# Attention by native float32 matmuls and TensorE transposes, in place of split products and DMA transposes

## The chip, the cores and the metric

The kernel runs on one core of one Trainium2 chip. The metric is device time in microseconds (us) of one execution; less is better. The core's engines are TensorE (PE, with its weight loads as PEld), VectorE (DVE), ScalarE (ACT), GpSimd (POOL) and SyncE (SP), whose queue issues the DMAs.

## What is computed

Sliding-window attention with a linear distance penalty, then two gated blocks, all in float32:

```python
scores = q @ k.T / sqrt(64)                      # 4 batches, 8 heads, 576 positions, 64 features
rel = pos[:, None] - pos[None, :]
scores = where((rel >= 0) & (rel < 128), scores - slope[h] * abs(rel), -1e9)
attn = exp(scores - max); attn = attn / (sum + 1e-9)
x = attn @ v                                     # as 2304 tokens x 512
x = ((x @ w_a) * (x @ w_b)) @ w_out              # inner width 1536
return (((x @ w1) * (x @ w2)) @ w3) @ w_out2     # inner width 1024
```

## The kernel before

Attention goes unit by unit: a unit is one batch and two heads, 16 in all, and the two heads fill the 128 partitions with their 64 features each. Its 576 queries are five blocks i, four of 128 and a last one of 64, where both heads share the partitions. The window lets block i see keys of blocks i - 1 and i alone, so a softmax piece (one block, one head) has 128 columns for i = 0 and 256 after; the last block is one piece for both heads. `RUNS` makes three steps of a unit: blocks 0 and 1, blocks 2 and 3, block 4. "Wide" steps are the first two.

For the next unit, `prep` transposes the ten 128x128 blocks of q and k on TensorE in three parts of three, four and three (L269, with `ident`), and `parted` moves each part to SBUF as a float32r high part (ACT, L273) and the remainder (DVE, L274). `v_parts` makes three bfloat16 parts of v on GpSimd. `scores` sums three products of q's and k's parts (low x high, high x low, high x high) in PSUM (L312); for the four full blocks the two heads are two matmuls of 64 rows each, in the upper and lower half of the array. `exps` adds the bias with a running minimum of the negated score on DVE (L338) and takes exponential and row sum on ACT (L344). `norms` makes 2^15 over the row sum (L357, L360). `probs` writes the divided exponentials as float16 high part (ACT L376, for block 0 DVE L372) and float16 remainder (DVE L378), and one DMA transpose from SP's queue turns both (L383). `pv` multiplies with v stationary, head j into PSUM partitions 64 j to 64 j + 63, five products per block of keys (L409); `pv_out` writes high and low part of x (ACT L423, DVE L424).

`attention_ops` lists the order of a step n: what the last step left for late (`parted`, `pv_out`), scores and exps of step n, norms and probs of step n - 1, loads, transposes of the next unit, then at most 2.4 us worth (`FILL`) of matmuls of the first gate group, then `pv` of step n - LAG. The `Filler` may run a tile of 256 tokens only when all four units of its batch have left `pv_out` (`ready`), when the first weight group is converted, and below a cut of the accumulator (1280 tokens, 1792 from the last batch on). In the first three units `keep_warm` adds two matmuls of 512 columns per full block (L353). Conversions of weights (`convert`: ACT L107, L110, DVE L114, L117, L121, POOL L126) run beside it, half a turn per step in the first batch, one turn after. After the loop come the rest of the filler (L546 and L572), the second weight group's conversion, and all later groups (L546, L583, L598) beside the conversion and multiplication of w3 with the last weight (L454, L462). PSUM in the attention part: three "s" tiles for scores, three "tr" tiles shared by transposes and `pv`, two "mm" tiles. A tile framework assigns the order on each engine and the waits.

## Time and profile before

| | us |
|---|---|
| median of 3 runs (995.44 to 999.41) | 998.87 |
| the profiled execution | 995.97 |
| its span, first to last instruction | 994.2 |
| mean granted TensorE clock in it | 0.979 |
| PE, DVE, ACT, POOL busy | 953.7, 533.0, 430.4, 399.5 |

A group of rows below is one view of the trace of the profiled execution. Times are from the span's start. Busy time of an engine is the union of its instructions; those of one engine overlap at their ends. A granted clock of 1.00 is 2.4 GHz; the other level is 1.2 GHz.

### The profile page before, as it was taken

How to read it: one execution, taken by the hardware profiler on the slowest of the kernel's cores; microseconds unless marked ns; L12 is line 12 of the kernel's file. 1: busy time of each engine (PE TensorE's matmuls, PEld its weight loads, DVE VectorE, ACT ScalarE, POOL GpSimd, SP SyncE). 2: the span in 40 equal slices, each digit the busy share in tenths (PEclk: the TensorE clock that was granted, in tenths of full speed). 3: DMA queues.
4: the chain of work that ended last, by engine and by line, in shares of the span. 5: the costliest groups of instructions: out<-in, count | busy, mean ns of one | idle time of the engine just before them, and what ended most of it. 6: DMA issues, size and time to landing. Idle time of an engine off the chain costs nothing.

```text
span 994.2 us, 16251 instructions
## 1 busy us (share of the span) xinstructions
PE 953.7 (96%) x6162; PEld 802.6 (81%) x6162; DVE 533.0 (54%) x1188; ACT 430.4 (43%) x1003; POOL 399.5 (40%) x329
## 2 busy tenths in 40 slices
PE   8889898888999999999999999999999999999998
PEld 6558787777988788888888888888888888888886
DVE  5979877775689734566474463442442442422222
ACT  5768867775554434434443342343421321311110
POOL 4344122221688423545362362584741631611111
PEclk9968999998999999999999999999999999999999
DMA  5797786764433222323341240120120120000012
GB/s 131 163 185 154 140 140 134 141 127 85 134 121 106 85 96 84 108 75 106 97 126 59 69 139 22 43 85 1 42 85 1 51 78 1 22 1 1 26 65 101
DMA packets 160079, 85.21 MB, mean 86 GB/s; under 512 B 128001, under 2 KB 148993, under 8 KB 160001
## 3 DMA queue, kind: packets, MB, share of 16 engines
q1 hardware_dynamic: 160000, 84.18, 34.1%
q8 instruction: 48, 0.79, 0.3%
q14 instruction: 31, 0.25, 0.1%
HBM read 58.20 MB, written 8.91 MB: 68 GB/s over the span
## 4 chain that ended last, share of the span: by engine, by line
PE 79%; DMA 7%; DVE 6%; ACT 3%; issue 3%; POOL 1%; SPq 1%; POOLq 0%; ACTq 0%; DVEq 0%
PE mm L546 44%; PE mm L583 11%; PE mm L598 10%; PE mm L462 4%; DMA pt<-pp 4%; PE s L312 3%; PE tr L409 3%; PE tr L269 2%; DVE pp L378 1%; PE mm L572 1%; DVE ca L121 1%; DMA raw<-in_moe_w_a 1%; DVE ca L117 1%; POOL ca L126 1%; PE mm L454 1%
## 5 line engine op out<-in xcount | busy, mean ns | idle before, releaser
L72 POOL TENSOR_TENSOR gl<-g,gh 128x512 fp32r<-128x512 f32 (+1 forms) x108 | 123.9, 1148 | 312.4 <-ACT gh L556 312.1
L553 DVE TENSOR_TENSOR g<-a,mm 128x512 f32<-128x512 f32 (+1 forms) x108 | 64.1, 594 | 212.8 <-PE mm L546 189.8
L126 POOL TENSOR_TENSOR ca<-ca,ce 128x512 int32<-128x512 int32 x76 | 101.3, 1333 | 141.2 <-ACT ce L110 68.6
L556 ACT ACTIVATE gh<-g 128x512 fp32r<-128x512 f32 (+1 forms) x108 | 60.2, 558 | 175.6 <-DVE g L553 175.6
L546 PE MATMUL mm<-x_hi,wlA 128*128 128x512 f32 (+1 forms) x464 | 107.5, 350 | 0.0
L551 ACT ACTIVATE a<-mm 128x512 f32<-128x512 f32 (+1 forms) x108 | 56.0, 519 | 117.5 <-PE mm L546 117.4
L546 PE MATMUL mm<-x_lo,whA 128*128 128x512 f32 (+1 forms) x464 | 104.0, 345 | 0.0
L546 PE MATMUL mm<-x_hi,whA 128*128 128x512 f32 (+1 forms) x464 | 102.9, 343 | 0.0
L546 PE MATMUL mm<-x_hi,wlB 128*128 128x512 f32 (+1 forms) x400 | 99.1, 370 | 2.1 <-DVE g L553 0.8
L546 PE MATMUL mm<-x_lo,whB 128*128 128x512 f32 (+1 forms) x400 | 98.5, 368 | 0.0
L546 PE MATMUL mm<-x_hi,whB 128*128 128x512 f32 (+1 forms) x400 | 98.1, 368 | 0.0
L114 DVE TENSOR_SCALAR ca<-ca 128x512 f32<-128x512 f32 x76 | 46.3, 610 | 91.8 <-ACT ca L107 90.6
L546 PEld LDWEIGHTS mm<-x_lo,whA 128*128 128x128 f32 x464 | 78.1, 192 | 10.5
L546 PEld LDWEIGHTS mm<-x_hi,wlA 128*128 128x128 f32 x464 | 77.7, 192 | 10.8 <-issue 0.4
L546 PEld LDWEIGHTS mm<-x_hi,whA 128*128 128x128 f32 x464 | 77.3, 191 | 10.2
L546 PEld LDWEIGHTS mm<-x_hi,wlB 128*128 128x128 f32 x400 | 70.8, 188 | 15.6 <-ACT a L551 1.3
L107 ACT ACTIVATE ca<-raw 128x512 f32<-128x512 f32 x76 | 50.7, 668 | 72.1 <-DMA raw<-in_moe_w 38.2
L587 DVE TENSOR_TENSOR acc<-acc,mm 128x512 f32<-128x512 f32 (+1 forms) x100 | 61.9, 629 | 36.9 <-PE mm L583 36.6
L546 PEld LDWEIGHTS mm<-x_lo,whB 128*128 128x128 f32 x400 | 71.1, 189 | 12.6
L546 PEld LDWEIGHTS mm<-x_hi,whB 128*128 128x128 f32 x400 | 71.0, 189 | 12.5
L121 DVE SCALAR_TENSOR_TENSOR ca<-raw,ca 128x512 int32<-128x512 int32 x76 | 79.9, 1052 | 1.8
L110 ACT ACTIVATE ce<-raw 128x512 int32<-128x512 uint32 x76 | 50.9, 670 | 60.0 <-POOL ca L126 24.9
(104 smaller groups left out, 1868.7 us busy)
## 6 DMA issues: line engine op xcount, KB each, us to landing
raw<-in_moe_w SPq DMA_DIRECT2D x32, 512.0 KB, 3.7
raw<-in_moe_w_out SPq DMA_DIRECT2D x20, 512.0 KB, 3.6
raw<-in_moe_w_a SPq DMA_DIRECT2D x12, 512.0 KB, 3.6
raw<-in_moe_w_b SPq DMA_DIRECT2D x12, 512.0 KB, 3.6
out<-acc SPq DMA_DIRECT2D x18, 256.0 KB, 2.0
q_raw<-in_q SPq DMA_DIRECT2D x32, 128.0 KB, 2.9
k_raw<-in_k SPq DMA_DIRECT2D x32, 128.0 KB, 2.7
v_raw<-in_v SPq DMA_DIRECT2D x32, 128.0 KB, 2.9
```

Source lines behind the costliest of these rows:

```text
L72: eng.tensor_tensor(out=out, in0=a, in1=b, op=ALU.subtract)
L107: nc.scalar.activation(a, f32(hw), ACTF.Abs)
L110: nc.scalar.activation(e, lw, ACTF.Copy, scale=2.0 ** -29)
L121: nc.vector.scalar_tensor_tensor(out=ai, in0=hw, scalar=-(1 << 30), in1=ai, op0=ALU.bitwise_and, op1=ALU.bitwise_or)
L126: nc.gpsimd.tensor_tensor(out=ai, in0=ai, in1=es[0], op=ALU.add)
L546: nc.tensor.matmul(p, w[:, z, kk, :], x[:, kk, o], start=(y == 0), stop=(y == len(terms) - 1))
L551: nc.scalar.activation(a, ps[0], ACTF.Copy)
L553: nc.vector.tensor_tensor(out=gg, in0=a, in1=ps[1], op=ALU.mult)
L556: nc.scalar.activation(gh, gg, ACTF.Copy)
L583: nc.tensor.matmul(p, w, x, start=(y == 0), stop=(y == len(terms) - 1))
L587: nc.vector.tensor_tensor(out=ya, in0=ya, in1=p, op=ALU.add)
L598: nc.tensor.matmul(p, x, w, start=(y == 0), stop=(y == len(terms) - 1))
```

## The change

`parted` moves each transposed part of q and k once, as plain float32, on DVE or (middle part) ACT. `scores` makes one native float32 product per block and head in place of three. `v_parts` goes; `pv` takes v as loaded. `norms` now also divides the exponentials in place on DVE, 1e-9 added to the sum as before and no 2^15. `probs` transposes them on TensorE into a "tr" tile, 128 columns at a time, and one copy moves the whole block: DVE for the first and the last block of a unit, ACT for the others. `pv` has one product per block of keys. LAG is 2 instead of 3. The warming matmuls read a constant tile of zeros.

```diff
-LAG = 3
+LAG = 2
+PES, PTS = 6, 6
...
+    def evict(eng, out, in_):
+        if eng is nc.scalar:
+            eng.activation(out, in_, ACTF.Copy)
+        else:
+            eng.tensor_copy(out=out, in_=in_)
...
             def parted():
-                hi, lo = qk[u]
-                nc.scalar.activation(hi[:, o], hold[0], ACTF.Copy)
-                nc.vector.tensor_tensor(out=lo[:, o], in0=hold[0], in1=f32(hi[:, o]), op=ALU.subtract)
+                evict(nc.scalar if n == 1 else nc.vector, qk[u][:, o], hold[0])
...
-        def v_parts():
...
-            sub(nc.gpsimd, r1, vr, upper[0])
-            sub(nc.gpsimd, v2, r1, upper[1])
...
-            for x, (a, b) in enumerate(((lo, hi), (hi, lo), (hi, hi))):
-                for j in range(nj):
-                    r = slice(j * D, (j + 1) * D) if nj == 2 else slice(0, P)
-                    nc.tensor.matmul(
-                        ps[j][:, at:at + n], a[r, qs], b[r, ks], start=(x == 0), stop=(x == 2)
-                    )
+            for j in range(nj):
+                r = slice(j * D, (j + 1) * D) if nj == 2 else slice(0, P)
+                nc.tensor.matmul(ps[j][:, at:at + n], t[r, qs], t[r, ks], start=True, stop=True)
...
+    def norms(run):
+        st = live.pop(run)
+        nc.vector.tensor_scalar(out=st[:, 2], in0=st[:, 1], scalar1=1.0e-9, scalar2=None, op0=ALU.add)
+        nc.vector.reciprocal(out=st[:, 3], in_=st[:, 2])
+        for u, i in run:
+            m, n, nb, nj = window(i)
+            d = live[u, i]
+            for j in range(nj):
+                pe = d["pe"][:, j, :n]
+                nc.vector.tensor_scalar(
+                    out=pe, in0=pe, scalar1=d["st"][:, 3, j:j + 1], scalar2=None, op0=ALU.mult
+                )
...
     def probs(u, i):
         m, n, nb, nj = window(i)
         d = live[u, i]
...
+        pe = d.pop("pe")
+        ps = ps_t.tile([P, W], F32, name="tr")[:, 0:nj * n]
         for j in range(nj):
...
-        nc.sync.dma_start_transpose(
-            out=t.rearrange("p (g m) -> p g m", m=P), in_=pp.rearrange("p a b c -> p (a b c)")
-        )
...
+            for g in range(nb):
+                o = (j * nb + g) * P
+                nc.tensor.transpose(ps[:, o:o + P], pe[:, j, g * P:(g + 1) * P], ident)
+        t = d["pt"] = sm_p.tile([P, W], F32, name="pt", bufs=PTS)[:, 0:nj * n]
+        evict(nc.vector if i in (0, NB - 1) else nc.scalar, t, ps)
...
-                for g in range(nb) for hl, z in ((0, 2), (1, 1), (1, 0), (0, 1), (0, 0))
...
+            for g in range(nb):
                 for j in range(2):
                     c = slice(j * D, (j + 1) * D)
+                    q0 = (j * nb + g) * P if nj == 2 else g * P + j * LAST
                     nc.tensor.matmul(
-                        ps[c, at:at + m], vs[z][:, kb, c], pt[:, j, hl, g, :],
-                        start=(x == 0), stop=(x == len(terms) - 1),
+                        ps[c, at:at + m], v_raws[u % 3][:, max(i - 1, 0) + g, c], t[:, q0:q0 + m],
+                        start=(g == 0), stop=(g == nb - 1),
                     )
...
-                keep_warm(WARM, t[:, 0:4 * P])
+                keep_warm(WARM, warm)
...
-            if k == RU - 1 and u + 1 < NU:
-                ops.append(trans[RU][0])
```

## Rows read from the trace of the kernel before

**Rows 1.** Stretches: us; PE, PEld, DVE, ACT, POOL busy; granted clock; DMA share, GB/s.

```profile
13.00:64.00 51.00, 42.49 (x405) 28.95 (x404) 44.01 (x151) 38.48 (x117) 15.94 (x12) 0.87 0.84 168
64.00:125.00 61.00, 56.19 (x673) 47.59 (x674) 51.97 (x187) 47.71 (x150) 21.46 (x19) 0.89 0.79 149
125.00:188.00 63.00, 54.84 (x718) 48.22 (x717) 48.06 (x177) 45.81 (x148) 14.92 (x14) 0.95 0.77 138
188.00:250.00 62.00, 52.31 (x712) 46.12 (x712) 38.41 (x156) 39.93 (x127) 11.08 (x11) 0.94 0.57 111
250.00:325.00 75.00, 73.26 (x432) 64.68 (x431) 60.11 (x71) 41.57 (x79) 56.49 (x42) 1.00 0.41 126
325.00:994.20 669.20, 664.63 (x3184) 559.18 (x3184) 284.99 (x423) 211.38 (x372) 268.72 (x213) 1.00 0.19 61
```

**Rows 2.** Chain of waits, 0 to 250 us: shares; then pieces (start, us, what).

```profile
by line: DMA pt<-pp 15.8%; PE mm L546 13.0%; PE s L312 11.8%; PE tr L409 10.2%; PE tr L269 7.1%; DVE pp L378 5.6%; PE mm L572 5.1%; issue 4.8%; DVE pe L338 2.6%; DMA k_raw<-in_k 2.5%; SPq L236 2.2%; ACT pp L376 2.2%; DMA q_raw<-in_q 2.1%; D
...
17.01 2.52 DMA pt<-pp
...
175.03 5.07 DMA pt<-pp
...
230.50 3.99 DMA pt<-pp
```

**Rows 3.** Groups by line and shape: out<-in, count, busy us, mean ns, idle before.

```profile
L378 DVE SCALAR_TENSOR_TENSOR pp<-pe,st,pp 128x256 f16<-128x256 f32 x112 | 61.5, 586 | 6.4 <-ACT pp L376 6.2
...
L376 ACT ACTIVATE pp<-pe,st 128x256 f16<-128x256 f32 x112 | 49.4, 500 | 8.8 <-DMA pt<-pp 6.1 <-ACT pe L344 0.9 <-DVE st L360 0.8
...
L274 DVE TENSOR_TENSOR qkl<-tr,qkh 128x384 fp32r<-128x384 f32 x32 | 17.6, 549 | 5.6 <-ACT qkh L273 5.5
...
L273 ACT ACTIVATE qkh<-tr 128x384 fp32r<-128x384 f32 x32 | 15.4, 482 | 12.1 <-PE tr L269 12.0
...
L378 DVE SCALAR_TENSOR_TENSOR pp<-pe,st,pp 128x128 f16<-128x128 f32 x32 | 11.8, 391 | 0.0
...
L274 DVE TENSOR_TENSOR qkl<-tr,qkh 128x512 fp32r<-128x512 f32 x16 | 10.9, 681 | 2.1 <-ACT qkh L273 1.9
...
L273 ACT ACTIVATE qkh<-tr 128x512 fp32r<-128x512 f32 x16 | 9.4, 589 | 6.6 <-PE tr L269 6.6
...
L372 DVE TENSOR_SCALAR pp<-pe,st 128x128 f16<-128x128 f32 x32 | 8.1, 291 | 2.2 <-DMA pt<-pp 2.0
```

**Rows 4.** One line's instructions (ns min/median/max), and two groups as in Rows 3.

```profile
L114 DVE TENSOR_SCALAR ca<-ca x76: 414/428/1511, 37.1 to 856.5; 128x512 f32<-128x512 f32 x76
...
L551 ACT ACTIVATE a<-mm 128x512 f32<-128x512 f32 x72 | 42.5, 592 | 92.5 <-PE mm L546 92.5
...
L424 DVE SCALAR_TENSOR_TENSOR x_lo<-tr,x_hi 128x256 fp32r<-128x256 f32 x32 | 13.2, 414 | 4.6 <-ACT x_hi L423 4.6
```

**Rows 5.** Timeline of PE near 156 us: start us, us, instructions merged.

```profile
155.94 0.28 PE L312 MATMUL s<-qkh 64*128 64x128 f32 x2
156.05 0.33 PE L312 MATMUL s<-qkh,qkl 64*128 64x256 f32 x2
156.22 0.28 PE L312 MATMUL s<-qkl,qkh 64*128 64x256 f32 x2
156.34 0.28 PE L312 MATMUL s<-qkh 64*128 64x256 f32 x2
```

**Rows 6.** Chain of waits near 26 and 210 us: start, us, what.

```profile
26.57 0.97 PE mm L353 x2
...
207.91 1.24 PE tr L409 x40
...
210.09 1.43 PE mm L572 x12
211.52 2.88 PE mm L546 x24
```

**Rows 7.** Timeline of PE near 343 us: start us, us, instructions merged.

```profile
343.25 0.60 PE L454 MATMUL mm<-ident,ca 128*128 128x128 f32 x4
343.61 0.71 PE L462 MATMUL mm<-oh,w3l 128*128 128x512 f32 x2
```

**Rows 8.** Clock in 40 slices (tenths); timeline of PE near 39 us, idle in brackets.

```profile
PEclk9968999998999999999999999999999999999999
...
39.66 0.30 PE L409 MATMUL tr<-pt,v 128*64 128x128 f16 x4 [2.95 <-DVE st L357]
```

More of the change, by code (lines that the diff above doesn't have):

```diff
@@ L188, in attention_moe_moe @@
     v_raws = [raw_p.tile([P, NB, P], F32, name=f"v_raw{i}") for i in range(3)]
+    warm = raw_p.tile([P, W], F16, name="warm")
     def consts():
@@ L264, in trans @@
                 if n == 0:
-                    qk[u] = [tr_p.tile([P, 2 * NB * P], F32R, name=f"qk{x}") for x in "hl"]
+                    qk[u] = tr_p.tile([P, 2 * NB * P], F32, name="qk")
                 ps = ps_t.tile([P, W], F32, name="tr")[:, 0:o.stop - o.start]
@@ L271, in parted @@
             def parted():
-                hi, lo = qk[u]
-                nc.scalar.activation(hi[:, o], hold[0], ACTF.Copy)
-                nc.vector.tensor_tensor(out=lo[:, o], in0=hold[0], in1=f32(hi[:, o]), op=ALU.subtract)
+                evict(nc.scalar if n == 1 else nc.vector, qk[u][:, o], hold[0])
             return trans, parted
-        def v_parts():
-            vr = v_raws[u % 3]
-            r1 = tr_p.tile([P, NB, P], F32, name="v1")
-            v2 = tr_p.tile([P, NB, P], BF16, name="v2")
-            upper = [t.bitcast(BF16).rearrange("p c (f t) -> p c f t", t=2)[:, :, :, 1] for t in (vr, r1)]
-            vS[u] = upper + [v2]
-            sub(nc.gpsimd, r1, vr, upper[0])
-            sub(nc.gpsimd, v2, r1, upper[1])
-        return [part(n) for n in range(len(parts))] + [(v_parts, None)]
+        return [part(n) for n in range(len(parts))]
     live = {}
@@ L333, in step_exps @@
         ps = d.pop("ps")
-        pe = d["pe"] = sm_p.tile([P, 2, 2 * P], F32, name="pe", bufs=5)
+        pe = d["pe"] = sm_p.tile([P, 2, 2 * P], F32, name="pe", bufs=PES)
         st = d["st"]
@@ L353, in keep_warm @@
             nc.tensor.matmul(ps[:, :x.shape[1]], x[:, 0:P], x, start=(y == 0), stop=(y == cnt - 1))
-    def norms(run):
-        st = live.pop(run)
-        nc.vector.tensor_scalar(
-            out=st[:, 2], in0=st[:, 1], scalar1=1.0e-9, scalar2=1.0 / PSC, op0=ALU.add, op1=ALU.mult
-        )
-        nc.vector.reciprocal(out=st[:, 3], in_=st[:, 2])
     def probs(u, i):
@@ L422, in pv_out @@
         ps = outs.pop(run)[:, :m]
-        nc.scalar.activation(x_hi[:, hp, o], ps, ACTF.Copy, scale=1.0 / PSC)
-        nc.vector.scalar_tensor_tensor(
-            out=x_lo[:, hp, o], in0=ps, scalar=1.0 / PSC, in1=f32(x_hi[:, hp, o]),
-            op0=ALU.mult, op1=ALU.subtract,
-        )
+        nc.scalar.activation(x_hi[:, hp, o], ps, ACTF.Copy)
+        sub(nc.vector, x_lo[:, hp, o], ps, f32(x_hi[:, hp, o]))
         if hp == NP - 1:
@@ L732, in attention_moe_moe @@
     fl = Filler()
[L733 removed]
     nc.vector.memset(warm, 0.0)
[L735 removed]
+    keep_warm(10, warm[:, 0:2 * P])
     paid = 0.0
```

46 lines of the change are left out of this document (9 added, 37 removed).

## Prediction

> **What bounds the kernel now.** I read the table of stretches first [rows 1]. From 325 us to the end PE is busy 664.63 of 669.20 us at a granted clock of 1.00, on the later product groups, which the change doesn't touch. The 75 us before that convert the second weight group and finish the filler; there DVE and POOL lead, and nothing of it is edited. The four middle stretches, 13 to 250 us, hold the attention loop, about one batch each, 51, 61, 63 and 62 us. Only these 237 us and the 13 us ahead of them can move, so the reader should forget the page's "PE 96%" and ask what limits a batch.
>
> Second view: the chain of waits over 0 to 250 us [rows 2]. Its largest single item is the DMA transpose of the probabilities, 15.8% of 250 us or 39.5 us, in pieces of up to 5.07 us. DVE's split of the probabilities (L378) adds 5.6%. In the first batch DVE is busy 44.01 of 51 us, 86%: the fullest that any vector engine gets in this loop, and my measure of how full the leading engine can be there. In the later batches DVE falls to 85%, 76% and 62% while the cadence stays at 61 to 63 us, so there waits decide, the DMA transposes first. PE's busy column counts overlapped matmuls and waits for nothing useful here; I count its work by start-to-start times instead.
>
> **What goes from DVE and ACT.** A unit (one batch, two heads) has nine softmax pieces, seven of 256 columns and two of 128; there are 16 units. By the groups' busy totals [rows 3], DVE loses L378 (61.5 + 11.8 us), L372 (8.1) and L274 (17.6 + 10.9): 109.9 us, 6.9 per unit. It gains the division of each piece in place, two evictions of transposed q and k, and two of transposed probabilities. The division reads and writes float32 in SBUF with a scalar; the nearest row is L114, 0.428 us median for 512 columns and 1.511 at most [rows 4]. For 256 columns I bound it by 0.21 (half the median) and 0.59 (the mean of L378, which it replaces) and take 0.30, near half of L114 plus a fixed part; 0.20 for 128. That is 7 x 0.30 + 2 x 0.20 = 2.5 us. The q and k copies of 384 columns from PSUM are priced as L274's 0.55, the probability copies of 256 as L424's 0.41 [rows 3, 4]: 2 x 0.55 + 2 x 0.41 = 1.9. Net on DVE: 6.9 - 4.4 = 2.5 us less per unit, 10 per batch; with 0.59 for the division it is only 0.5 less.
> ACT loses L376 (49.4) and L273 (15.4 + 9.4): 74.2 us, 4.6 per unit; it gains one q/k copy of 512 columns and three probability copies of 512, each 0.59 as L551 [rows 3, 4]: 2.4. Net 2.2 less per unit. GpSimd loses the two v subtractions of each unit; it is the least loaded engine in these stretches [rows 1], so I cost that at nothing. SP loses 80 transposes that stand in its queue ahead of the q, k and v loads; that gain is inside the 39.5 us of waits and isn't counted again.
>
> **What PE gets.** Prices at the full clock.
> Scores: with float32r, two 64-row matmuls (heads j = 0 and 1) start together, and pairs follow each other after 0.11 to 0.17 us, 0.113 typically, whether they have 128 or 256 columns [rows 5]. A unit has five such groups (four pairs and the full-row last block) times three terms: 15 x 0.113 = 1.70 us.
> Output product: 40 matmuls take 1.24 us, 0.031 each or 0.062 a pair [rows 6]; a unit has 90, 2.79 us (the last block's narrower ones priced alike). Transposes: four of 128 columns last 0.60 us, the next matmul starting 0.36 us after the first [rows 7]; between 0.09 and 0.15 each, I take 0.11. Ten for q and k are 1.1 us. Sum before: 5.6 us per unit.
> A native float32 matmul is in no row. Low end: the price of one float32r pass. High end: four passes, with nothing of a pair side by side. I take four passes with the pairs still overlapped: the old code forms a full product from two-part numbers by three of the four partial products (it drops low x low), and the native form owes all four. So scores 5 x 4 x 0.113 = 2.26 us, output 9 pairs x 4 x 0.062 = 2.23, q/k transposes 1.1, and the new ones of the probabilities, 16 per unit (2 + 3 x 4 + 2), 1.76. Sum after: 7.35 us, 1.75 more per unit, 28 us more PE work in all.
> The Trainium skill, FP8 and Floating Point Precision, section TensorE Precision Notes, says that true float32 makes four passes through the array. No run so far shows it; by it the sum would be the one I make.
>
> **The sum.** Filler of the first gate group runs from the second batch on. A tile costs 48 matmuls of L546 and 24 of L572, 2 x 2.88 + 2 x 1.43 = 8.6 us [rows 6]; readiness and the accumulator cuts let six tiles through before the loop's end, 17.2 us per batch. So PE holds 4 x 5.6 + 17.2 = 39.6 us in each of these batches now, and 4 x 7.35 + 17.2 = 46.6 after. DVE after: 34, 42, 38 and 28 us. PE becomes the leader. At 86% full: 46.6 / 0.86 = 54 us instead of 61, 63 and 62. In the first batch there is no filler but 24 warming matmuls, 0.97 us for two early on [rows 6], about half of that at twice the clock, together 6 to 12, say 9 us: PE 4 x 7.35 + 9 = 38.4, / 0.86 = 45 instead of 51. The loop: 45 + 3 x 54 = 207 against 237, 30 us less.
> At the ends the pipe is one step shorter (LAG 2), and the transposes in the first fill (2.52 us) and the drain (3.99) [rows 2] give way to a PE transpose and a copy of about 1.2 us each: 4 us less. The tail from 250 us on is shifted, not shortened. 995.97 (the profiled execution) - 34 = 962; the median of the three runs lies 2.9 above that execution, so 965.
> A new wait: the transposes of a piece on PE wait for its division, which stands on DVE behind the next step's four bias-and-maximum operations, and the copies then stand on ACT behind the next exponentials. Behind the waiting transposes PE has q/k transposes, an output product and, from the second batch, 2.4 us of filler per step; I cost it at nothing beyond the 14% idle that the fullness already allows. Without that cover it costs up to 2 us in each of 32 wide steps. The copies also bring the ring of three "tr" PSUM tiles from two to four tiles per wide step.
>
> **The rivals.**
> Slower: the passes of a pair don't overlap. Two 64-row or two 64-column native matmuls then run one after the other: scores 9 x 4 x 0.113 = 4.1, output 18 x 4 x 0.062 = 4.5, transposes 2.9; 11.4 us per unit. Batches: (45.6 + 17.2) / 0.86 = 73 us, the first (45.6 + 9) / 0.86 = 63; 283 against 237, so 1041. It decides from about 9.0 us per unit on (53 us of PE work fill 62 us at 86%). For it: a matmul that is several passes long may hold the order. Against: pairs do overlap in both forms now [rows 5, 6].
> No change: only one pass in four of a pair overlaps, since PE starts matmuls in order. A pair costs six passes: 3.2 + 3.3 + 2.9 = 9.4 us per unit, 64 us per batch and 54 in the first; 1003.
> Better: a native matmul costs about one pass. Then PE has 4.0 us per unit, DVE leads again with 34 / 0.86, 42 / 0.86 and 38 / 0.86, and the loop is about 172 us: 929.
> Clock: the table has 0.87 to 0.95 of the clock in the loop [rows 1], and the slices show 0.6 at the worst [rows 8]; the fall there came after PE sat idle 2.95 us. If the loop ran at 0.65, PE's 46.6 us would be 72 and a batch 83: about 1085. Against it, the stretch from 325 us holds transposes too, at 1.00, and the change makes PE denser. The Trainium skill, TensorE: Matmul & The Clock Gate, Part 4, says that transposes don't count as activity for the clock gate, which speaks against this change with its 256 more; the late stretch doesn't show that harm, since its 64 transposes are few.
>
> **How the numbers follow.** The forecast (945 to 985) 0.57, better 0.10, no overlap 0.13, partial overlap 0.17, clock 0.03. The range 938 to 1006 leaves out no overlap, clock and the lower part of "better", under 0.2. About 0.5% is what a measurement of this kernel can tell from no change. Faster: 0.57 + 0.10 + 0.03 of partial = 0.70; same: 0.10 of partial; slower: 0.13 + 0.03 + 0.04 = 0.20.
>
> **What would show it.** Right: the two matmuls of a score pair starting within a few ns; about 0.45 us per score pair; DVE's stretch in the first batch near 34 us busy; batches of 45 and 54 us; the stretch from 325 us shifted, not shorter; no DMA transpose in the chain. Wrong: a second head's matmul that starts only after the first's last pass; divisions of over 0.5 us; PE idle before the probability transposes with DVE as releaser; a clock under 0.85 in the loop.

## The result and the profile after

The changed kernel takes 986.47 us (median), 0.988 of the kernel before (95% interval 0.985 to 0.991). That median is of four executions, of which one took 1999.8 us, for no cause that the record shows, and is left out of the ratio; the other three lie from 984.28 to 987.53. The profiled execution is 987.53 us with a span of 985.7 us, beside 995.97 and 994.2: 8.4 us less where 34 were forecast (12.0 less by the means behind the ratio). The direction was right, the size was a quarter to a third of the forecast.

To see where the time went, both spans are cut where the last output product of each batch ends. That gives four batches and a tail; in the kernel before the cuts lie at 83.9, 141.3, 196.7 and 249.8 us, in the changed one at 80.9, 137.1, 188.9 and 240.0. First the kernel before, in the columns of [rows 1]: stretch, its length, then busy time (and count) of PE, PEld, DVE, ACT, POOL, then the granted clock and the DMA columns.

```profile
0.00:83.90 83.90, 70.45 (x626) 51.72 (x627) 65.37 (x233) 58.69 (x177) 33.24 (x36) 0.84 0.79 157
83.90:141.30 57.40, 52.18 (x677) 44.78 (x677) 48.13 (x177) 44.99 (x143) 17.32 (x16) 1.00 0.78 146
141.30:196.70 55.40, 48.47 (x640) 42.77 (x639) 42.86 (x157) 40.55 (x128) 13.05 (x13) 0.94 0.75 136
196.70:249.80 53.10, 44.49 (x609) 39.23 (x609) 31.50 (x128) 33.02 (x106) 10.69 (x11) 0.94 0.55 107
```

The same view of the changed kernel, with its late stretch, which answers to the last of [rows 1]:

```profile
0.00:80.90 80.90, 65.65 (x432) 45.65 (x433) 61.19 (x226) 49.21 (x144) 25.31 (x30) 0.83 0.60 152
80.90:137.10 56.20, 54.56 (x478) 44.93 (x479) 40.39 (x172) 36.67 (x118) 7.28 (x8) 1.00 0.29 65
137.10:188.90 51.80, 50.27 (x460) 41.95 (x461) 36.32 (x164) 33.91 (x112) 2.93 (x4) 1.00 0.26 59
188.90:240.00 51.10, 48.55 (x428) 41.09 (x429) 29.40 (x127) 28.95 (x93) 2.93 (x4) 0.93 0.16 36
...
315.00:985.70 670.70, 666.78 (x3208) 561.74 (x3206) 279.62 (x416) 207.80 (x365) 262.04 (x208) 1.00 0.18 59
```

Read the PE column against the length. In batches 2 to 4 of the kernel before TensorE is busy 52.18 of 57.40, 48.47 of 55.40 and 44.49 of 53.10 us: idle 5.2, 6.9 and 8.6. In the changed kernel it is idle 1.6, 1.5 and 2.6 us. The waits are gone, as forecast; but there had been only 20.7 us of them in three batches, and TensorE now has more to do.

A batch is split here into three terms that add up to its length: TensorE's work counted at full clock (busy time less half of the busy time in the stretches at 1.2 GHz), the clock's share (that half), and TensorE's idle time. Busy time runs to the modelled end of each matmul, so "work" also holds the gaps between shapes and about 0.2 us ahead of each wait. Us, each batch as work + clock + idle:

| | batch 1 | batch 2 | batch 3 | batch 4 | tail |
|---|---|---|---|---|---|
| before | 83.9 = 57.7 + 12.8 + 13.4 | 57.4 = 52.2 + 0 + 5.2 | 55.4 = 45.1 + 3.4 + 6.9 | 53.1 = 41.5 + 3.0 + 8.6 | 744.4 |
| after | 80.9 = 53.2 + 12.5 + 15.2 | 56.2 = 54.6 + 0 + 1.6 | 51.8 = 50.3 + 0 + 1.5 | 51.1 = 45.4 + 3.1 + 2.6 | 745.7 |

Batch 1 holds the start and, since scores run ahead of outputs, about five units of scores; batch 4 holds three. Whole spans, split alike: before 994.2 = 934.5 + 19.2 + 40.5, after 985.7 = 940.5 + 17.2 + 27.9.

By kind of matmul, work in the four batches at full clock (from each start to the next, or to its own end), beside what the prediction's prices come to for 16 units, us:

| | before: forecast | before: measured | after: forecast | after: measured |
|---|---|---|---|---|
| scores | 27.2 | 53.0 | 36.2 | 42.7 |
| output product | 44.6 | 45.8 | 35.7 | 35.7 |
| transposes of q and k | 17.6 | 24.4 | 17.6 | 20.6 |
| transposes of probabilities | - | - | 28.2 | 31.0 |

The sum was to grow by 28 us and grew by 7: the old scores cost nearly twice their price, so the native scores took work away rather than added it.

The chain of waits, 0 to 240 us of the changed kernel, shares by line (to be read beside [rows 2]):

```profile
by line: PE mm L521 16.1%; PE s L306 14.8%; PE tr L368 11.5%; PE tr L387 10.9%; PE mm L547 7.8%; PE tr L276 6.1%; DVE pe L350 4.0%; ACT pe L336 3.9%; DVE pe L330 3.2%; PE mm L358 2.7%; issue 2.0%; DMA raw<-in_moe_w_a 1.8%; DVE st L343 1.7%;
```

The DMA transpose, first there with 15.8%, has no place in it. Line numbers have moved: the scores are L306, the division L350, the new transposes L368, the output product L387, the transposes of q and k L276, the filler L521 and L547.

The new prices, in the timeline of PE (start, us, instructions merged; a native float32 matmul is recorded as two weight loads and two matmuls):

```profile
141.10 0.88 PE L387 MATMUL tr<-pt,v_raw 128*64 128x128 f32 x12
141.91 0.93 PE L306 MATMUL s<-qk 64*128 64x128 f32 x8
142.76 0.39 PE L547 MATMUL mm<-gh,wlA 128*128 128x256 f32 x1
...
145.96 1.14 PE L306 MATMUL s<-qk 64*128 64x256 f32 x8
147.03 0.50 PE L547 MATMUL mm<-gh,wlA 128*128 128x256 f32 x2
...
153.53 1.04 PE L368 MATMUL tr<-ident,pe 128*128 128x128 f32 x8
154.50 0.93 PE L306 MATMUL s<-qk 64*128 64x128 f32 x8
155.35 0.39 PE L521 MATMUL mm<-x_hi,wlA 128*128 128x256 f32 x1
```

Eight records at 145.96 are two score pairs of 256 columns, and the next line starts 1.06 us later, with a switch to another array shape at both ends; from a record of one pair to the same record of the next, without a switch, it is 0.43 us, where 0.45 was forecast. (At 154.50 the merged line holds a pair of 128 columns and one of 256, 0.85 us with both switches; a pair of 128 takes 0.22 without.) Twelve at 141.10 are three output pairs in 0.81 us, 0.27 with the switch to another array shape in it; between pairs of one run it is 0.22 (forecast 0.25). Eight transposes take 0.97 us, 0.12 with a switch, 0.108 to 0.109 between neighbours (forecast 0.11). The two heads of a pair start 6 to 7 ns apart where the program order puts them side by side, so such pairs do overlap. For scores it does so with 224 of 256 records here, but with only 286 of 384 in the kernel before; the other heads run one after the other.

The division and what waits for it (one line's instructions: ns min/median/max; then who waited, us and times):

```profile
L350 DVE TENSOR_SCALAR pe<-pe,st x144: 273/348/1430, 13.4 to 229.2; 128x256 f32<-128x256 f32 x112, 128x128 f32<-128x128 f32 x32
...
  PE tr L368: 4.3, 3
```

### The profile page after: what moved, and what is told of

The parts are those of the page before. It is cut to its first block, busy times and chain, and to the rows that moved or that the text cites. A ratio compares the mean times of both kernels' runs of the same rounds, so it can differ in the third digit from the quotient of the medians.

```text
span 985.7 us, 14334 instructions
## 1 busy us (share of the span) xinstructions
PE 957.8 (97%) x5410; PEld 798.7 (81%) x5410; DVE 507.3 (51%) x1172; ACT 398.4 (40%) x907; POOL 358.7 (36%) x297
## 4 chain that ended last, share of the span: by engine, by line
PE 86%; DVE 7%; ACT 2%; DMA 2%; issue 1%; SPq 1%; POOL 0%; ACTq 0%; DVEq 0%
PE mm L521 46%; PE mm L558 12%; PE mm L573 10%; PE mm L437 4%; PE s L306 4%; PE tr L368 3%; PE tr L387 3%; PE mm L547 2%; PE tr L276 1%; DVE ca L114 1%; DVE ca L117 1%; DVE pe L350 1%; ACT pe L336 1%; DVE ca L121 1%; DVE pe L330 1%
## 5 line engine op out<-in xcount | busy, mean ns | idle before, releaser
L521 PE MATMUL mm<-x_hi,wlA 128*128 128x512 f32 (+1 forms) x464 | 109.7, 351 | 1.1 <-DVE g L528 1.1
L521 PE MATMUL mm<-x_lo,whA 128*128 128x512 f32 (+1 forms) x464 | 104.4, 345 | 0.0
L521 PE MATMUL mm<-x_hi,whA 128*128 128x512 f32 (+1 forms) x464 | 102.8, 343 | 0.0
L521 PE MATMUL mm<-x_hi,wlB 128*128 128x512 f32 (+1 forms) x400 | 99.2, 370 | 0.0
L521 PE MATMUL mm<-x_lo,whB 128*128 128x512 f32 (+1 forms) x400 | 98.6, 368 | 0.0
L521 PE MATMUL mm<-x_hi,whB 128*128 128x512 f32 (+1 forms) x400 | 98.1, 368 | 0.0
L114 DVE TENSOR_SCALAR ca<-ca 128x512 f32<-128x512 f32 x76 | 52.2, 686 | 83.8 <-ACT ca L107 83.7
L521 PEld LDWEIGHTS mm<-x_hi,wlA 128*128 128x128 f32 x464 | 77.8, 190 | 13.4 <-issue 1.5
L521 PEld LDWEIGHTS mm<-x_lo,whA 128*128 128x128 f32 x464 | 77.9, 191 | 10.3 <-issue 0.2
L521 PEld LDWEIGHTS mm<-x_hi,whA 128*128 128x128 f32 x464 | 77.2, 190 | 10.4 <-issue 0.3
L336 ACT ACTIVATE pe<-pe,st 128x256 f32<-128x256 f32 (+1 forms) x144 | 68.1, 474 | 35.8 <-DVE st L330 35.5
L521 PEld LDWEIGHTS mm<-x_hi,wlB 128*128 128x128 f32 x400 | 71.6, 190 | 12.7
L521 PEld LDWEIGHTS mm<-x_lo,whB 128*128 128x128 f32 x400 | 71.1, 189 | 12.5
L521 PEld LDWEIGHTS mm<-x_hi,whB 128*128 128x128 f32 x400 | 71.0, 189 | 12.4
L121 DVE SCALAR_TENSOR_TENSOR ca<-raw,ca 128x512 int32<-128x512 int32 x76 | 75.7, 996 | 1.9
```

The costliest lines, as they stand in the source:

```text
L114: nc.vector.tensor_scalar(out=a, in0=a, scalar1=bits(0x38000000), scalar2=None, op0=ALU.max)
L121: nc.vector.scalar_tensor_tensor(out=ai, in0=hw, scalar=-(1 << 30), in1=ai, op0=ALU.bitwise_and, op1=ALU.bitwise_or)
L336: nc.scalar.activation(pe[:, j, :n], pe[:, j, :n], ACTF.Exp, bias=st[:, 0, j:j + 1], scale=-1.0, accum_out=st[:, 1, j:j + 1],)
L521: nc.tensor.matmul(p, w[:, z, kk, :], x[:, kk, o], start=(y == 0), stop=(y == len(terms) - 1))
```

## The experiments

Sixteen kernels, each measured beside the kernel before (whose medians then lay between 996.1 and 997.9 us). The batches are cut as above, in the one profiled execution of each; "low" is the time at 1.2 GHz over the whole span, mean of the runs, worked out as (1 - mean granted clock) x 2 x span, since the clock shows only 1.0 and 0.5 here. "Held" means that memory is reserved, see the first experiment.

| kernel | median us | ratio, 95% | batches 1 to 4, us | tail | low, us |
|---|---|---|---|---|---|
| changed kernel | 986.47 | 0.985 to 0.991 | 80.9, 56.2, 51.8, 51.1 | 745.7 | 34 |
| 1 held 24.5 KB | 978.77 | 0.981 to 0.984 | 75.9, 55.9, 51.8, 49.8 | 746.2 | 20 |
| 2 division by a constant | 978.66 | 0.981 to 0.984 | 83.0, 52.5, 49.7, 42.9 | 749.8 | 22 |
| 3 one key block | 977.16 | 0.980 to 0.983 | 82.1, 51.0, 49.6, 49.4 | 744.2 | 38 |
| 4 more warming | 995.34 | 0.998 to 1.001 | 92.7, 53.6, 51.9, 51.5 | 745.4 | 23 |
| 5 native scores alone | 995.14 | 0.996 to 1.001 | 80.1, 63.6, 54.9, 50.5 | 744.5 | 47 |
| 6 second half alone | 997.16 | 0.997 to 1.002 | 87.4, 55.5, 53.2, 47.4 | 749.6 | 44 |
| 7 held, no warming | 983.08 | 0.982 to 0.989 | 77.4, 56.6, 51.6, 48.5 | 746.8 | 22 |
| 8 before, lag 4 | 1008.07 | 1.007 to 1.012 | 95.2, 65.2, 54.0, 46.3 | 746.7 | 64 |
| 9 held, lag 3 | 977.42 | 0.978 to 0.981 | 78.8, 53.6, 52.9, 40.2 | 751.1 | 15 |
| 10 held, less filler | 989.44 | 0.990 to 0.994 | 75.0, 52.9, 46.4, 38.8 | 774.3 | 24 |
| 11 before, less filler | 1017.58 | 1.017 to 1.022 | 84.0, 53.2, 54.2, 47.5 | 777.0 | 86 |
| 12 held, warming moved | 979.25 | 0.978 to 0.983 | 74.5, 57.1, 51.8, 49.9 | 744.5 | 18 |
| 13 warming moved | 987.57 | 0.987 to 0.993 | 78.8, 56.2, 51.8, 49.8 | 745.3 | 36 |
| 14 no warming | 984.82 | 0.986 to 0.990 | 77.5, 58.5, 51.8, 50.4 | 745.3 | 34 |
| 15 held 2 KB | 977.63 | 0.979 to 0.983 | 73.4, 56.3, 51.7, 51.2 | 744.4 | 16 |
| 16 changed kernel again | 987.52 | 0.988 to 0.993 | 82.5, 56.2, 51.8, 49.8 | 745.8 | 38 |

**1. Conversions kept out of the first batches.** The changed kernel needs less memory, and three conversions of the second weight group (three DVE operations each, L114 to L121) therefore stand in its first batch, at 33 to 42 us, nine in the loop in place of six. A reserved tile restores the old place.

```diff
+    raw_p.tile([P, 6272], F32, name="hold")
```

> The changed kernel with 24.5 KB per partition set aside for the length of the attention loop, so that the conversion buffers of the second weight group have no room inside it. Theory D (DVE leads the first batch; three conversions of the second weight group that moved into it at 34 to 52 us hold DVE there, about 1.4 us each without waits, more with them): the first batch, to its last output product, falls from 81 us by 4 to 7 us, the three later ones (56, 52, 51 us) don't change, and the end comes 3 to 6 us earlier if the later stage takes the conversions back for nothing, as it seems to, since the stretch after the loop is 746 us with the early conversions and 745 without. Theory C (the low granted clock of TensorE leads the first batch): first batch within 1.5 us of 81, total unchanged or up to 3 us more.

Measured: 978.77 us, first batch 5.0 us shorter as theory D had it, batch 4 by 1.3, the others and the tail nearly as they were. The conversions done early don't shorten the tail; they cost about 8 us. How they cost it is the subject of 12 to 16.

**2. Division by a constant.** The division by the row sum is left out, and with it the wait for the sum and the operand that differs by partition.

```diff
-   out=pe, in0=pe, scalar1=d["st"][:, 3, j:j + 1], scalar2=None, op0=ALU.mult
+   out=pe, in0=pe, scalar1=0.5, scalar2=None, op0=ALU.mult
```

> The changed kernel with the exponentials multiplied by the constant 0.5 in place of the per-row reciprocal, so the division by the row sum is left out. If a constant lets the operation run at the rate of the 512-column conversion step (0.428 us, about two columns per ns-scale cycle), 256 columns take about 0.29 us in place of 0.35 and follow each other after 0.2 us or less in place of 0.26. Theory D (DVE leads the first batch): first batch shorter by about 45 x 0.1 = 3 to 5 us, later batches the same within 1 us each, total -3 to -6. Theory P (TensorE leads everywhere): total unchanged within 2 us. If the operation takes 0.35 us here too, the rate is not set by the per-row scalar.

Measured: 978.66 us, 7.8 less, which neither theory had. The first batch did not become shorter (83.0), though VectorE was busy there for 56.9 us rather than 61.2; TensorE's idle time even rose from 15.2 to 20.4 us. The later batches did, in part because 34 of the 337 matmuls of the filler's first product (L521) moved behind the loop (tail 4.1 us longer). Less load on VectorE alone does not shorten the first batch. The instruction became as fast as expected: 0.286 us in the median for 256 columns, in place of 0.349.

**3. Output product with one key block.** Only the query's own key block is multiplied, five output pairs per unit in place of nine.

```diff
-            for g in range(nb):
+            for g in range(nb - 1, nb):
```

> The changed kernel with only the block's own keys in the output product; the older key block is left out there. Eight of 18 matmuls go per unit, four pairs of 0.22 us, 0.88 us of TensorE work per unit. Theory P (TensorE leads batches two to four at about 86% full): each of them 4 x 0.88 / 0.86 = 4.1 us shorter, 52 and 48 and 47 us, and the first batch (DVE leads) unchanged within 1.5 us: total -10 to -14. Theory W (round trips between DVE and TensorE lead there, the matmuls fill gaps): each later batch less than 1.5 us shorter, total -1 to -4.

Measured: batches 2 to 4 shorter by 5.2, 2.2 and 1.7 us, while TensorE's work in them fell by 5.1, 2.9 and 2.7 (4 x 4 x 0.22 = 3.5 of it taken out of each); in the first batch the work fell by 3.6 us and the idle time rose by 5.4. TensorE's work sets the later batches and not the first. The total fell by 9.3 us, just short of theory P.

**4. More warming products.** Six per output block in four units, in place of two in three.

```diff
-WARM_UNITS, WARM = 3, 2
+WARM_UNITS, WARM = 4, 6
```

> The changed kernel with six warming matmuls per full block in the first four units in place of two in the first three. Theory C (the low clock leads the first batch, 27 us of it granted 1.2 GHz): mean granted clock of the first batch rises from 0.80 to over 0.93 and the batch falls from 81 us by 4 or more. Theory D (DVE leads): the clock rises, the batch changes by less than 2 us either way.

Measured: the clock's share of the first batch fell from 12.5 to 5.8 us, its work rose by 16.9, and the batch grew by 11.8. The clock can be bought with products, at more than it is worth; neither expectation had that.

**5 and 6. Each half alone.** In 5 the kernel before gets native scores, with one copy of q and k, and nothing else. In 6 the changed kernel goes back to the split of q and k and to three score products; division, TensorE transposes and native output product stay. Six conversions lie in the loop in both.

```diff
-            for x, (a, b) in enumerate(((lo, hi), (hi, lo), (hi, hi))):
-                for j in range(nj):
...
+            for j in range(nj):
+                nc.tensor.matmul(ps[j][:, at:at + n], t[r, qs], t[r, ks], start=True, stop=True)
```

> The kernel before with the first half of the change alone: q and k are moved once as float32 and the scores are one native product; division, halves and DMA transposes stay. Like the kernel before it takes six conversions into the batches. Theory W (the gain of the change is the end of the waits for DMA transposes; in the kernel before TensorE stands idle 5.2, 6.9 and 8.6 us in batches 2 to 4, mostly ahead of the output product): this half leaves these waits, and it makes a score pair dearer (0.43 for 3 x 0.113 us), so 995 to 1000 us beside about 997 of before, batches 2 to 4 within 1 us of 57.4, 55.4 and 53.1. Theory L (any load taken off VectorE and ScalarE shortens a batch; this half takes 2.7 us per batch off VectorE and 3.9 off ScalarE): 2 to 3 us per batch, so 986 to 990 us.

> The changed kernel with the first half undone: q and k are split in two and the scores are three products again; the division, the TensorE transposes and the native output product stay. Six conversions lie in the batches, as in the kernel before and in the one with held memory (978.8 us). Theory W: nearly all of the gain without the moved conversions (about 18 us) is here: 978 to 984 us, batches 2 to 4 near 56, 52 and 50 us. Theory L: VectorE keeps 2.7 us per batch and ScalarE 3.9, so about half of the gain: 986 to 990 us.

Measured: neither moves the time (995.14 and 997.16), while both together, in the held kernel, give 18 us. For 5 this is what the waits let one expect, though its second batch was not: 63.6 us. For 6 all expectations missed. The first two batches of 5, then of 6:

```profile
0.00:80.10 80.10, 60.24 (x587) 40.20 (x587) 65.22 (x229) 54.30 (x167) 33.39 (x36) 0.85 0.76 159
80.10:143.70 63.60, 56.00 (x634) 45.53 (x631) 45.95 (x174) 42.37 (x134) 17.84 (x16) 0.89 0.72 143
```

```profile
0.00:87.40 87.40, 73.81 (x489) 53.62 (x490) 59.73 (x228) 52.78 (x153) 24.10 (x30) 0.77 0.45 111
87.40:142.90 55.50, 54.19 (x506) 45.95 (x507) 39.31 (x169) 38.14 (x122) 3.44 (x5) 1.00 0.29 65
```

In 6 the waits of batches 2 and 3 are gone (54.19 busy of 55.50), so it is the second half that removes them, as expected; but its first batch runs at 0.77 of the clock, 41 us at 1.2 GHz, against 20.5 in the held kernel. Half of TensorE's busy time there is 18.9 us against 8.8: that is 10 of the 11.5 us by which its first batch is longer. In 5 the second batch has 13.7 us at the low clock, which is 6.8 by the split. Neither theory had the clock in it. Over the whole span, as work + clock + idle, 5 is 922.2 + 25.8 + 45.6 and 6 is 946.3 + 20.5 + 26.3, beside 934.5 + 19.2 + 40.5 before: native scores alone take 12 us of work away and idle time and clock fill it again; the second half alone takes 14 us of idle time away and puts 12 of work in its place. Only together do they leave something.

**7. No warming in the held kernel.**

```diff
-WARM_UNITS, WARM = 3, 2
+WARM_UNITS, WARM = 0, 2
```

> The kernel with held memory (978.8 us, batches 75.9, 55.9, 51.8, 49.8) without the warming products in the first three units (24 products of 512 columns, about 0.22 us each at full clock, 5.3 us; the ten at the start stay). If TensorE's work in the first batch is on the path and the clock is not worth its price: first batch 71 to 74 us, total 973 to 977. If the warming holds the clock up: the granted clock of the first batch falls from 0.87 to below 0.8 and the first batch grows by 2 to 6 us, total 981 to 985.

Measured: 4.6 us less work in the first batch, 6.4 us more idle, the same 20.5 us at the low clock. The few warming products lie in TensorE's waits and cost nothing; without them the kernel is 4.3 us slower. The second expectation's total came (983.08), but not its reason, since the clock did not fall.

**8. Before, with a longer lag.** `LAG = 4` in place of 3. (With this lag the last output product of a pair of heads reads the v of a later pair.)

```diff
-LAG = 3
+LAG = 4
```

> The kernel before with the output product four steps behind the scores rather than three, so that a DMA transpose has one more step (about 4.5 us) to land; nothing else is changed. If the waits of the output product for the DMA transposes were latency alone (2.0 to 4.5 us too late at a time), they go and the kernel gains what the change itself gains or more in batches 2 to 4: 982 to 988 us. If the step behind only moves the wait (the same buffers, five and six, now come free later, so that the next halves wait for the output product): 995 to 1003 us.

Measured: slower than both expectations. In batches 3 and 4 the idle time did fall, to 3.4 and 5.2 us, but in the first it rose from 13.4 to 22.7, and the low clock from 61 to 64 us over the span. Late in the loop a longer lag hides waits, at its start it adds some; which waits these are was not traced.

**9. The lag back to three, in the held kernel.**

```diff
-LAG = 2
-PES, PTS = 6, 6
+LAG = 3
+PES, PTS = 6, 7
```

> The kernel with held memory with the output product three steps behind the scores, as in the kernel before, rather than two (and one more buffer for the moved probabilities; the held memory a little smaller, six conversions as before). Theory E: batches 2 to 4 do not move by more than 1 us, since TensorE is full there; the first batch, which has idle time, can move by 3 us either way; total 976 to 982. If the short lag was itself a source of the gain: total above 984.

Measured: 977.42 us, within 2 us of the held kernel. The order of work shifts between the batches and the tail (batch 4 is 9.6 us shorter, so the expectation for single batches missed), the total hardly. The shorter lag was no source of the gain. This kernel and number 15 (977.63) are the fastest that leave no work out; both beat the kernel before and the changed one.

**10 and 11. Filler moved behind the loop**, in the held kernel and in the kernel before.

```diff
-FILL = 2.4
+FILL = 0.6
```

> The kernel with held memory (978.8 us; batches 75.9, 55.9, 51.8, 49.8) with filler paid 0.6 us per step in place of 2.4: some 10 us of the gate's products per batch move from batches 2 to 4 to the time after the loop, nothing is left out. Theory E (in batches 2 to 4 TensorE is busy 95 to 99% and only its work counts, so work is worth the same wherever it stands): batches near 46, 42 and 40 us, the tail 28 to 30 us longer, the total within 3 us of 978.8. Theory W (waits of the attention chain set the pace and the filler lies in them): batches 2 to 4 stay within 3 us, the tail grows all the same, total 995 to 1008.

> The kernel before (about 996 us; batches 83.9, 57.5, 55.3, 53.2, TensorE idle 5.2, 6.9 and 8.6 us in the last three) with filler paid 0.6 us per step in place of 2.4, nothing left out. Theory E says that this kernel, unlike the changed one, was not bound by TensorE: its batches shrink by less than what is moved out of them (by 3 to 6 us each for some 10), the tail takes all of it, total 1005 to 1020. If it was bound by TensorE's work as well: total within 3 us of 996.

Batches 2 to 4 of the held kernel with less filler, then of the kernel before with less:

```profile
75.00:127.90 52.90, 52.49 (x466) 43.11 (x464) 40.37 (x175) 35.58 (x118) 5.51 (x6) 1.00 0.30 68
127.90:174.30 46.40, 43.74 (x392) 34.19 (x391) 36.22 (x163) 30.54 (x105) 2.20 (x3) 1.00 0.29 65
174.30:213.10 38.80, 33.47 (x302) 24.53 (x301) 26.58 (x123) 23.98 (x80) 0.00 (x0) 0.96 0.21 47
```

```profile
84.00:137.20 53.20, 48.29 (x643) 40.45 (x643) 44.34 (x163) 40.96 (x131) 16.98 (x15) 1.00 0.76 146
137.20:191.40 54.20, 43.08 (x566) 34.80 (x562) 44.31 (x165) 38.80 (x130) 12.40 (x11) 0.87 0.77 143
191.40:238.90 47.50, 36.51 (x506) 30.73 (x502) 32.74 (x127) 29.08 (x96) 7.85 (x6) 0.75 0.73 125
```

By the split used above, 23.4 us of work left the three batches of the held kernel, and they became 19.4 us shorter: 0.83 us for each. In the kernel before 26.5 us left and 11.0 came back, 0.42 for each; idle time (11.1 and 11.0 us in batches 3 and 4) and low clock (0.87, 0.75) took the rest. The tails grew by 28.1 and 32.6 us. So the change did turn a loop paced by waits into one paced, mostly, by TensorE's work. The held kernel's total (989.44) lay between the two expectations: with the filler gone, waits show again in its fourth batch (33.47 of 38.80). Number 11 (1017.58) came as expected of a kernel that TensorE does not bound.

**12 to 16. Conversions in or out, three times.** 12 moves the 24 warming products of the held kernel ahead of the new transposes; 13 is 12 without held memory, 14 is 7 without it, 15 holds 2 KB only, 16 is the changed kernel again.

```diff
     def probs(u, i):
         m, n, nb, nj = window(i)
+        if u < WARM_UNITS and m == P:
+            keep_warm(WARM, warm)
...
-            if u < WARM_UNITS and m == P:
-                keep_warm(WARM, warm)
```

> The kernel with held memory (978.8 us, first batch 75.9 us with 14.7 us of TensorE idle and 20.5 us at the low clock) with the same 24 warming products ahead of the probability transposes of the first three units, where TensorE waits for divisions, rather than behind their output products. Theory C (what is left to gain in the first batch is the low clock, some 0.45 us for each us of it): idle falls to 8 to 12 us, the time at the low clock below 14 us, total 973 to 977. If the clock does not follow from where this idle time lies: low clock within 4 us of 20.5 and total 977 to 982.

> The kernel with the warming products ahead of the transposes (979.25 us; first batch 74.5, 13.7 us of it at the low clock, TensorE idle 16.8), without the held memory, so that three more conversions lie in the first batches (nine for six). Theory D (these conversions load VectorE in the first batch and delay the divisions): total 984 to 988 us, TensorE idle in the first batch 3 us or more above 16.8. Theory C (they cost only through the granted clock): total above 979 by 0.45 us for each us that the time at the low clock grows, idle within 2 us of 16.8. Theory N (the pair of 986.5 and 978.8 us was a chance of the order): total within 3 us of 979.25.

> The kernel without warming products (983.08 us; first batch 77.4, low clock 20.5 us, TensorE idle 21.1), without the held memory: nine conversions for six. Theory D: 988 to 992 us, TensorE idle 24 us or more. Theory C: low clock longer and 0.45 us for each us of it, idle within 2 us of 21.1. Theory N: within 3 us of 983.

> The changed kernel with only 2 KB per partition held, enough to keep the three conversions out; the order of instructions is that of the kernel with 24.5 KB held (978.77 us). Theories D and C: 977 to 981 us, low clock about 20 us over the whole span. If the amount or the place of the memory mattered: elsewhere.

> The changed kernel itself once more, beside the three others (986.47 us; first batch 80.9, low clock 27.3 us there, idle 15.2). All theories: 984 to 988 us; theory C adds that its time at the low clock is again 30 to 38 us over the span, 10 to 18 us above that of the held kernel, and that 0.45 us for each us of it accounts for the difference within 2 us.

The first batches of 15 and 16, then of 12 and 13, each without and with the three conversions:

```profile
0.00:73.40 73.40, 58.37 (x426) 40.72 (x426) 55.47 (x213) 44.36 (x133) 21.35 (x27) 0.91 0.54 132
```

```profile
0.00:82.50 82.50, 67.89 (x432) 47.03 (x433) 61.20 (x226) 49.33 (x144) 25.30 (x30) 0.79 0.59 149
```

```profile
0.00:74.50 74.50, 57.70 (x426) 40.14 (x426) 54.82 (x211) 43.86 (x130) 21.29 (x27) 0.91 0.54 130
```

```profile
0.00:78.80 78.80, 64.73 (x432) 45.18 (x433) 61.95 (x226) 49.28 (x144) 24.99 (x30) 0.85 0.62 156
```

VectorE has 6 to 7 us more with the conversions, yet TensorE's idle time is not longer: 15.0 and 14.6 us, 16.8 and 14.1. What differs is the clock: 0.91 against 0.79, 0.91 against 0.85. The means of the runs:

| kernel | conversions | span, us | low, us | span - 0.45 x low |
|---|---|---|---|---|
| changed | 9 | 983.9 | 34.1 | 968.6 |
| 16 changed again | 9 | 985.8 | 37.5 | 968.9 |
| 13 warming moved | 9 | 985.1 | 36.0 | 968.9 |
| 1 held 24.5 KB | 6 | 977.2 | 20.1 | 968.2 |
| 15 held 2 KB | 6 | 976.0 | 16.1 | 968.7 |
| 12 held, warming moved | 6 | 977.1 | 18.1 | 968.9 |
| 9 held, lag 3 | 6 | 975.2 | 14.6 | 968.7 |

0.45 is half of TensorE's busy share at the low clock (24.9 of 27.3 us in the changed kernel's first batch). With it the means of seven kernels agree within 0.7 us, so the clock can account for the 8 us that the conversions cost. That they cost it by plainly longer waits of TensorE, as my first theory for experiment 1 had it, falls. The pair without warming (7 and 14) is an exception: 981.5 and 982.9 us with 22.1 and 34.4 us low; there the idle time fell by 4.5 us as the clock's share rose by 5.3, and the totals differ by 1.7 us, as theory N had it.

The single executions don't bear the account out in full. The four of number 16 have 31.5 to 43.4 us at the low clock, yet their spans lie between 985.5 and 986.1 us; 0.45 would make 5 us of that. The four of 14 have 23.6 to 39.3 and differ by 1.5 us. In 4 and 6, with ten executions each, the span does move by 0.44 and 0.43 us per us. A straight line through the 27 executions of the seven kernels, with a term for the three conversions, gives 0.26 us per us (standard error 0.06) and leaves 3.7 us (1.2) to the conversions themselves. So the clock is a part of what they cost; how large a part is not settled.

Of the other expectations, 12 met neither: its low clock in the first batch fell to 13.7 us as theory C wanted, but TensorE's idle time rose to 16.8 and the total stayed (979.25). Numbers 13, 15 and 16 came within the totals of theory C, 13 with 2.7 us less idle time than 12, where the theory allowed 2.

What stood ahead of the first three falls, in stretches of the changed kernel cut where its clock changes, but for the first (columns as above):

```profile
22.90:29.70 6.80, 2.50 (x27) 1.79 (x26) 3.96 (x19) 3.52 (x12) 0.00 (x0) 1.00 0.86 203
29.70:36.50 6.80, 5.70 (x32) 3.92 (x30) 6.07 (x20) 5.05 (x15) 3.32 (x3) 0.50 1.09 299
36.50:39.90 3.40, 1.88 (x19) 1.22 (x21) 3.33 (x10) 3.40 (x10) 1.54 (x2) 0.99 1.02 269
39.90:43.40 3.50, 3.50 (x16) 2.26 (x14) 3.50 (x7) 1.87 (x4) 2.39 (x2) 0.51 0.73 196
43.40:46.80 3.40, 1.30 (x18) 0.89 (x16) 3.40 (x13) 1.40 (x6) 1.27 (x1) 1.00 0.32 124
46.80:60.40 13.60, 12.28 (x58) 8.17 (x60) 9.54 (x34) 9.64 (x27) 3.83 (x3) 0.50 0.54 142
```

Each of these falls to 0.50 (1.2 GHz) follows a stretch in which TensorE was idle for much of the time: 2.50 busy of 6.80 us, 1.88 of 3.40, 1.30 of 3.40. The batch's fourth fall, at 67.3 us, follows 5.06 busy of 6.90. In the last two of the three DVE is full (3.33 and 3.40 of 3.40), and the conversions at 33 to 42 us lie ahead of them or in them. So it may be that they put waits of TensorE at places where its clock then falls, and that the slower products after that fill what would have been idle time; this fits the rows and was not tested by itself. Why the split scores of experiment 6 bring still more of the low clock stays open.

In the kernel before the time at the low clock hardly moves the total: over 50 runs its low time lay between 42 and 80 us, and its span moved by 0.05 us for each us of it. That its waits absorb the slower products is argued from the idle time in its batches; a run of it at the full clock was not made.

## Why the prediction was right or wrong

- **What bounds the kernel: the failed step.** "PE's busy column counts overlapped matmuls and waits for nothing useful here; I count its work by start-to-start times instead" threw away the one column that held the answer. [rows 1] show TensorE idle for 4.8, 8.2 and 9.7 us in the three stretches from 64 to 250 us: 22.7 us was all that the end of every wait could give there, before any new work. The prices from single pieces came to 39.6 us of work per batch; measured at full clock it was 52.2, 45.1 and 41.5. Scores took 11.6 us in batch 3 and 12.4 in batch 2 (from each start to the next) where 4 x 1.70 = 6.8 stood, the filler 19.3 and 22.9 where 17.2 stood; the output product (11.5 to 12.4 for 11.2) and the transposes of q and k (5.3 for 4.4) were nearer. The gaps of 0.113 us between like pairs leave out the switch between array shapes, about 0.1 us more each time, and the heads that don't start side by side (98 of 384 records). In batch 2, at full clock, 48 switches account for 6.0 of the 12.6 us that were missing, and 23 filler matmuls more than the two tiles of the sum for 2.8; the rest is spread.
- **The difference of work.** For the same reason the "28 us more PE work in all" was wrong: 7 came, since the old scores, priced at 27, had cost 53, and the native ones, at 43, were cheaper. It was luck that this error ran the kernel's way: over the whole span 14.6 us of idle time and clock went, which 28 us of new work would have outweighed.
- **The base of the difference.** The stretches of 61, 63 and 62 us were taken for batches; cut by the last output product, batches 2 to 4 were 57.4, 55.4 and 53.1. Against the forecast's 67 us of waits in them (186 less three times 39.6) stood 20.7 us of idle time and 6.4 of clock.
- **The batch after.** 54 us each was forecast; 56.2, 51.8 and 51.1 came, 53.0 in the mean. Two errors cancel in it: 46.6 us of work where 50.1 were (at full clock, mean of the three), and 86% full where the rows show 95 to 97%. The 86% was the fullness of DVE in the first batch of the old kernel, and nothing tied it to TensorE in the new one. So batches 2 to 4 gave 6.8 us rather than 24: 18.3 us of idle time and clock went, 11.5 us of work came.
- **First batch.** 45 for a stretch of 51 us was forecast; it lost 3.0 of 83.9. Its length is 53.2 us of work, 12.5 of clock and 15.2 of idle time, where the sum had 38.4 us of work at 86% full for a shorter stretch and no term for the clock. It also took in three conversions that the sum knew nothing of: the smaller tiles let other work move forward, which cost about 8 us (1.7 without the warming products). The sentence that the tail is "shifted, not shortened" held, even for them (745.7 and 744.4 us).
- **Ends.** 4 us less was forecast for start and drain; the tail is 1.3 us longer (1.7 of it is the clock's share, of which the tail before has none), and the drain isn't seen as a gain in any batch; it was not measured by itself.
- **Prices of the new pieces: right.** Overlap within a pair and four passes: 0.43 us a pair of 256 columns and 0.22 one of 128 (the sum had 0.45 for both in the scores); a transpose took 0.108. The rule in the Trainium skill, FP8 and Floating Point Precision, section TensorE Precision Notes, that true float32 makes four passes, agrees: 0.43 us for 256 columns is four times their number at 2.4 GHz. So the rivals without overlap or with part of it fell, and "better" too.
- **DVE.** 10 us per batch less was forecast. Over the four batches it fell from 187.9 to 167.3 us of busy time, with about 6 us of early conversions in the latter: 6.5 less per batch. The division took 0.349 us in the median and 0.388 in the mean for 256 columns, above the 0.30 taken, inside the bounds. With 0.59 as the upper bound I had looked on it as the risk; experiment 2 shows that a shorter one doesn't shorten the first batch.

The divisions and copies that make up the new load of DVE, 0 to 240 us of the changed kernel (columns as in [rows 3]):

```profile
L350 DVE TENSOR_SCALAR pe<-pe,st 128x256 f32<-128x256 f32 x112 | 37.9, 388 | 0.6
L261 DVE COPY qk<-tr 128x384 f32<-128x384 f32 x32 | 17.8, 555 | 14.1 <-PE tr L276 14.0
L261 DVE COPY pt<-tr 128x256 f32<-128x256 f32 x32 | 13.4, 420 | 4.0 <-PE tr L368 3.8
...
L350 DVE TENSOR_SCALAR pe<-pe,st 128x128 f32<-128x128 f32 x32 | 8.6, 307 | 0.2
```

- **The new wait.** PE's transposes did wait for divisions, 4.3 us in three places over the whole loop, far less than the 2 us in each of 32 steps that was named as its price without cover. Longer were waits that the prediction named without a price, for the "tr" tiles in PSUM: transposes of q and k waited for the copy of probabilities, and the other way round, all in the first batch. The longest, 4.3 us, ends at 29.4 us, just ahead of the first fall of the clock. Who waited for whom, 0 to 240 us of the changed kernel (us in total, times, longest):

```profile
PE tr L276 <- DVE pt L261: 4.8, 2, 4.3
PE tr L368 <- DVE qk L261: 4.5, 2, 3.2
PE tr L368 <- DVE pe L350: 4.3, 3, 2.5
```

- **The clock.** The rival had 0.65 of the clock over the whole loop and 1085 us, which didn't happen: batches 2 and 3 ran at 1.00 with 64 new transposes in each. The rule of the Trainium skill, TensorE: Matmul & The Clock Gate, Part 4, that transposes don't count as activity, is thus not borne out as harm in those batches. But the first batch ran at 0.83 of the clock in the mean, under the 0.85 named as a sign of being wrong, and the forecast had no term for that: 34 to 38 us at 1.2 GHz over the span, by the split 17.2 us of the profiled execution. Against the kernel before, with 19.2, that is no loss; it shows only beside kernels with less of it, and there its price is not settled (see 12 to 16).

## What to carry to other kernels

Before you credit a change with the end of waits, take the idle time of the engine that will lead afterwards, stretch by stretch cut at the same event: that is the ceiling of the gain, and the added work of that engine comes off it. Check prices put together from single pieces against the busy column; if they give much less, the pieces lack something (here switches between array shapes, heads that did not start together, more filler), not the column. Check the work that is to go as closely as the work that is to come. When tiles shrink, look which other work an automatic order now moves forward, and once TensorE sets the pace, count the time at the low clock as a term of its own.

## What the runs showed of the hardware

- A native float32 matmul appears as two weight loads and two matmuls; two of them on halves of the array, next to each other in order, start 6 to 7 ns apart, and a pair costs 0.43 us for 256 moving columns (64 rows each), 0.22 for 128 (64 columns each).
- A matmul that follows one of another array shape starts about 0.1 us later than one of the same shape (0.202 to 0.209 us from start to start between a transpose or output product and a matmul of another shape, or a filler product and an output product, against 0.108 to 0.120 within one kind); batches 2 and 3 hold 101 such switches in the kernel before and 81 in the changed one.
- On DVE a float32 multiplication by a per-partition value costs a fixed 0.06 us more than one by a constant, at nearly the same rate per column: successive divisions start 0.263 us apart with 256 columns and 0.196 with 128, the multiplications by 0.5 of experiment 2 0.203 and 0.132. Single divisions reach 1.43 us; the seven of over 0.6 us all overlap a GpSimd operation.
- The time at the low clock can go with 0.43 to 0.44 us of span per us in one kernel (4 and 6, ten executions each) and with 0.05 in another (the kernel before, 50 executions; 16, four).
